# Swapped operands for the P product of twelve mLSTM units: values stationary, P streaming, the result turned back through DRAM

## The chip, the core and the metric

The kernel runs on one core of a Trainium2 chip. Its time is the device time of one execution in microseconds; the time of a version is the median of its runs. TensorE (PE in the profile) multiplies matrices into PSUM, with weight loads (PEld) as instructions of their own; VectorE (DVE), ScalarE (ACT) and GpSimd (POOL) do the element-wise work; SyncE (SP) issues most transfers (DMA).

## What is computed

An mLSTM cell over 4 batches, 8 heads, 768 steps and a head size of 40, followed by a wide MLP over its 3072 rows of 320 numbers. Everything is fp32. Cut to what matters:

```
for t in range(S):                                   # S = 768, for each of 4 x 8 heads
    m_new = max(f[t] + m, i[t])
    f_stab, i_stab = exp(f[t] + m - m_new), exp(i[t] - m_new)
    C = f_stab * C + i_stab * outer(v[t], k[t])      # 40 x 40
    n = f_stab * n + i_stab * k[t]                   # 40
    y[t] = sigmoid(o[t]) * (C @ q[t]) / max(abs(n @ q[t]), 1)
x = y as rows of (batch, step), 320 columns (8 heads x 40)
h = x @ w_in                                         # 320 -> 2048
out = (h - tanh(h)) @ w_out                          # 2048 -> 320
```

## The kernel before, in words

**Units.** The cell is done in chunks of 128 steps. A unit is one batch and one chunk with its 8 heads: 4 x 6 = 24 units, number n = chunk x 4 + batch. Within a unit, TensorE makes for each head the scores `ps` (keys against queries, 128x128, two heads at a time in the upper and lower 64 rows of the array), VectorE masks them into `P` (128 partitions are the source steps, the columns the target steps), and two kinds of products go into one PSUM tile `ph` (128 steps x 8 heads x 41; the 41st column is the denominator n·q):

- `inter` (line 654): what the state brings, three products per unit (three heads each, block-diagonal state), `ph<-state,q` in the profile;
- `intra` (line 663): what the steps of the chunk bring, one product per head, `ph<-vs,P`. `P` is the stationary operand (128x128), and the values `vs` of the head, scaled by the input gate in `scaled` (line 607) and with the scale itself as 41st column, stream through: 41 columns.

`gate` (line 668) reads `ph` on VectorE, makes the denominator `den`, multiplies it into the opened output gate `o`, and writes `ys`. `turn_by_store` (line 726) turns `ys` in blocks of 32x32 on VectorE into `yt`, stores that to DRAM (`y_rows`, four transfers) and loads it back as `xT` (two transfers), so that features lie on partitions. `update` makes `pc`, three products of keys and values, and `keep_state` adds them to the state on VectorE.

**MLP.** Two units make a group of 256 rows; there are 12 groups. For each group and each of 8 pairs of 128-wide strips of the hidden layer, `up` makes `ph_up` from `xT` and `w_in` (320 = 128 + 128 + 64: the 64-row rests run in pairs in the halves of the array), ScalarE and VectorE form h - tanh(h) from polynomials (`z`, `q`, `gt`), and `down_seven` multiplies `gt` and its sums `s` with `w_out` and `wT` into `pS`, seven products in place of eight. An item is two pairs of one group.

**Order.** The kernel pins the order of every engine to the order of its calls. Units 0 to 11 and the first four groups are laid out by a planner (`Plan`) with costs and ranks. From the item START = 17 on, 32 items follow in a loop written out by hand. In each item TensorE gets the `ph_up` products (with other work merged in), then the 64-row rests together with the scores of a new unit (`halves`), then the `pS` products of the item before. The work of units 12 to 23 is laid beside it in slots of two items: slot `(s, s - 1)` begins unit s and finishes the unit o = s - 1 before it; `cell_slot` (line 743) lists its steps, `spread_over` spreads them evenly over the two items, and `merge` (line 1031) sets them between the items' own steps. Work that waits for another engine is put off by `Clock.later` by so many microseconds of planned time.

**Buffers.** The `ph_up` tiles have two PSUM banks, used by every item, so that VectorE's first pass over them (`gt<-ph_up,z`) must be over before the next item's products start. The scores have the banks `a0` and `a1` to themselves. `ph` and `pc` share one bank in these slots. `P` has four buffers in SBUF, `vs` four, `yt` two.

In the profile every instruction carries the line of a helper that pins the order (L129 for TensorE, L106 for the others), so that the names of the tiles tell what it is. An fp32 product appears as two records of matmul and two of weight load.

Of the kernel before, what the change touches and what calls it, by code (L numbers as in the profile page):

```python
# [49 lines left out]
FP = mybir.dt.float32  # L50
# [5 lines left out]
OP = mybir.AluOpType  # L56
# [4 lines left out]
L = 128  # L61
# [18 lines left out]
def kernel(  # L80
# [188 lines left out]
    B, NT, D, H, _ = qT.shape  # L269
# [72 lines left out]
    def load_unit(n, names=("kz", "qz", "v", "k", "o", "q2"), queue=SP, behind=()):  # L342
        c, b = divmod(n, B)
        t = ld.setdefault(n, {})
        for name in names:
            if name in ("kz", "qz"):
                t[name] = load.tile([128, HH, L], FP, name=name, tag=name, bufs=3)
                for i in range(2):
                    src = kT if name == "kz" else qT
                    dma = queue.dma_start(out=t[name][i * HALF:i * HALF + D], in_=src[b, c, :, i * HH:(i + 1) * HH])  # L350
                    if behind:
                        tc.add_manual_dep(dma.ins, behind[-1].ins.name, SYNC, reason="order of transfers")
            elif name == "k":
                if n + B < NU:
                    t["k"] = load.tile([L, WIDE, D], FP, name="k", tag="k", bufs=3)
                    queue.dma_start(out=t["k"].rearrange("p h d -> p (h d)"),
                                    in_=bass.AP(k.tensor, k[b, c].offset, [[H * D, L], [1, WIDE * D]]))
            elif name != "q2":
                src, bufs = {"v": (v, 3), "o": (o_gate, 4)}[name]
                t[name] = load.tile([L, H, D], FP, name=name, tag=name, bufs=bufs)  # L360
                queue.dma_start(out=t[name], in_=src[b, c])
            elif c:
                t["q2"] = load.tile([TOP, len(TRIOS), L], FP, name="q2", tag="q2", bufs=3)
                for i in range(TRIO):
                    queue.dma_start(out=t["q2"][i * D:(i + 1) * D, 0:len(range(i, H, TRIO))], in_=qT[b, c, :, slice(i, H, TRIO)])
# [210 lines left out]
    def trio(t, j):  # L576

        return t[:, TRIOS[j].start:TRIOS[j].stop].rearrange("p h d -> p (h d)")
# [18 lines left out]
    def prepare(n, whole=True, by_heads=False):  # L597

        t = un[n]
        if "vs" in t:  # L600
            return
        t["vs"] = scaled(n, 0, "vs", 4, by_heads)
        if whole:
            t["column"]()
            open_gate(n)

    def scaled(n, i, name, bufs, by_heads=False):

        t = un[n]
        to = att.tile([L, H, D1], FP, name=name, tag=name, bufs=bufs)  # L610
        scale = ei[:, i, t["c"], t["hs"]]
        t["column"] = lambda: A.copy(out=to[:, :, D], in_=scale)
        if by_heads:
            for h in range(H):
                A.mul(out=to[:, h, 0:D], in_=t["v"][:, h], mul=scale[:, h:h + 1])
        else:
            V.tensor_tensor(out=to[:, :, 0:D], in0=t["v"], in1=scale.unsqueeze(2).to_broadcast([L, H, D]), op=OP.mult)
        return to
# [32 lines left out]

    def inter(n, j):
        t = un[n]
        if "ph" not in t:
            t["ph"] = small([L, H, D1], "ph")
        if t["c"]:
            rows = slice(0, len(TRIOS[j]) * D)
            T.matmul(trio(t["ph"], j), t["qs"][rows, j, :], trio(state[t["b"]][t["c"] % 2][rows], j), start=(j == 0), stop=False,  # L660
                     skip_group_check=True)

    def intra(n, h):
        t = un[n]
        T.matmul(t["ph"][:, h, :], t["P"][:, h // HH, h % HH, :], t["vs"][:, h, :], start=(t["c"] == 0 and h == 0), stop=True,
                 skip_group_check=True)

    def gate(n, in_parts=False):

        t = un[n]  # L670
        ph, sg = t["ph"], t["o"]
        den = att.tile([L, H], FP, name="den", tag="den")


        def over():
            V.scalar_tensor_tensor(out=den, in0=ph[:, :, D], scalar=-1.0, in1=inv[:, t["c"], t["hs"]], op0=OP.mult, op1=OP.max)
            V.tensor_tensor(out=den, in0=den, in1=ph[:, :, D], op=OP.max)
            V.reciprocal(out=den, in_=den)

        def shares():  # L680
            for h in range(H):
                A.mul(out=sg[:, h], in_=sg[:, h], mul=den[:, h:h + 1])

        def product():
            y = t["y"] = ys[n % 2]
            V.tensor_tensor(out=y.rearrange("p (h d) -> p h d", d=D), in0=ph[:, :, 0:D], in1=sg, op=OP.mult)

        if in_parts:
            return over, shares, product
        over()  # L690
        V.tensor_tensor(out=sg, in0=sg, in1=den.unsqueeze(2).to_broadcast([L, H, D]), op=OP.mult)
        product()

    def update(n, j, at_once=True):
        t = un[n]
        if j == 0:
            t["pc"] = small([TOP, H, D1], "pc")
        T.matmul(trio(t["pc"], j), t["k"][:, TRIO * j:TRIO * (j + 1)].rearrange("p h d -> p (h d)"), trio(t.get("vs_end", t["vs"]), j), start=True, stop=True)
        if j == len(TRIOS) - 1 and at_once:
            keep_state(n)  # L700
# [25 lines left out]
    def turn_by_store(n):  # L726

        y, g, tt = un[n]["y"], *divmod(n, GT)  # L730
        yt = att.tile([L, NB, BLOCK], FP, name="yt", tag="yt")
        flat = yt.rearrange("p b j -> p (b j)")
        V.transpose(flat[:, 0:NK * 128], y[:, 0:NK * 128])
        V.transpose(flat[:, NK * 128:], y[:, FROM[NK]:])
        rows = dram.tile([(NK + 1) * 128, L], FP, name="y_rows", tag=f"y_rows{n % 4}")
        for a in range(L // BLOCK):
            part = slice(a * BLOCK, (a + 1) * BLOCK)
            SP.dma_start(out=rows[:, part].rearrange("(b i) j -> i b j", i=BLOCK), in_=yt[part])
        for i in range(2):
            half = slice(i * HALF, (i + 1) * HALF)  # L740
            SP.dma_start(out=xT[g % NX][half, :, tt * L:(tt + 1) * L], in_=rows.rearrange("(c p) t -> p c t", p=128)[half])

    def cell_slot(s, o):


        steps, pause = [], [(0.0, lambda: None)]
        if o is not None:
            prepare(o)
        if s is not None:
            if s + 1 < NU and s + 1 not in ld:  # L750
                load_unit(s + 1)
            begin(s)
        if o is None:
            return [(0.0, lambda: prepare(s))]
        for d, heads in enumerate(TRIOS):
            steps.append((0.22 if o >= B else 0.0, lambda d=d: inter(o, d)))
            steps += [(0.22, lambda h=h: intra(o, h)) for h in heads]
        steps.append((0.0, lambda: gate(o)))
        steps += 5 * pause
        if o + B < NU:  # L760
            steps += [(0.2, lambda j=j: update(o, j)) for j in range(len(TRIOS))] + 4 * pause
        steps += [(0.0, lambda: turn_by_store(o))] + 2 * pause
        if s is not None:
            steps.append((0.0, lambda: prepare(s)))
        return steps + 2 * pause


    gT, po = {}, {}
# [624 lines left out]
        spread_over([(0.0, lambda p=p: [step() for _, step in sums_of_weights(p)])], START + p / 2, START + 0.5 + p / 2)  # L1393
    banks[:] = [name for name in ("b0", "b1") if name != third["tag"]]
    load_unit(PLANNED)
    for x in range(START, len(items) + LAG):
        dense, new = [], []
        for slot, x0, x1 in begins[x]:
            spread_over(cell_slot(*slot), x0, x1)
            if slot[0] is not None:  # L1400
                new.append(slot[0])
        if x < len(items):
            some = tuple(run[:2] for run in items[x])
            dense, rest = up(some, shrink(x))
            dense.append((0.6 + 0.9 * len(new[:1]), lambda: halves(rest, *(scores(n) for n in new[:1]))))
        dense += [(0.9, lambda n=n: halves(scores(n))) for n in new[1 if x < len(items) else 0:]]
        some = tuple(run[:2] for run in items[x - LAG])
        if in_seven(*some[0]):
            dense += down_seven(some)
        else:  # L1410
            for i, run in enumerate(items[x - LAG]):
                dense += down(i, some, *run)
        if x == len(items):
            dense.insert(4, (0.0, count))
            dense.insert(13, (0.0, load_count))
        merge(dense, [(at - x, cost, step) for at, cost, step in sorted(work[x], key=lambda w: w[0])])

    Clock.tick(100.0)
# [197 lines left out]
```

## Time and profile before

| | us |
|---|---|
| runs | 542.87, 531.3, 532.08 |
| median | 532.08 |
| the profiled execution: its own time | 542.49 |
| its span in the trace | 540.7 |
| TensorE busy in the span | 534.0 |
| VectorE busy | 361.5 |
| ScalarE busy | 199.8 |
| GpSimd busy | 35.8 |
| eight score products of a unit, first to last start of record and length | 218.21 to 219.20 |
| units 12 to 23: first scores to last product | about 214 to 472 |

The page of the profile gives for each engine the time in which one of its instructions ran. Matmuls are pipelined: the recorded length of one (0.3 to 0.4 us for the products here) reaches over the start of the next, so what a product costs TensorE is read from the starts of successive lines in the timeline and not from the length of a line. A line of the timeline merges consecutive records of one kind; its columns are start, length, engine, source line, operation, `output<-inputs`, shape and number of records.

### The profile page before, as it was taken

The numbers are of one execution on the slowest core, as the hardware profiler recorded it, in microseconds if no ns is written. First come the engines' busy times: TensorE is split into PE (matmuls) and PEld (weight loads), VectorE is DVE, ScalarE is ACT, GpSimd is POOL, SyncE is SP. The second block draws the span as 40 slices with busy tenths as digits, with TensorE's granted clock in tenths as the row PEclk, the third lists the DMA queues.
The fourth block names the chain that finished last, engine by engine and source line by source line (L and its number), as shares of the span: only waits on it lengthen the run. The fifth ranks groups of instructions, "written<-read, shape, count | busy, mean of one in ns | idle before, by whom it ended". The sixth has DMA issues, their size and how long they took to land.

```text
span 540.7 us, 9346 instructions
## 1 busy us (share of the span) xinstructions
PE 534.0 (99%) x3505; PEld 464.4 (86%) x3505; DVE 361.5 (67%) x792; ACT 199.8 (37%) x509; POOL 35.8 (7%) x63
## 2 busy tenths in 40 slices
PE   9999999999999999999999999999999999999996
PEld 5778888788888988898899899989989989988885
DVE  3678979998766557765756657557566566555544
ACT  4157487576543433232232242223223223222312
POOL 4421312310000000000000000000000000000000
PEclk9999999999999999999999999999999999999999
DMA  7966456551201000002132241241231221020001
GB/s 231 273 193 201 134 141 186 159 161 57 79 16 62 1 26 24 1 26 70 59 105 46 60 130 25 80 115 16 76 94 38 76 54 16 16 53 1 25 0 31
DMA packets 52331, 42.71 MB, mean 79 GB/s; under 512 B 23160, under 2 KB 46008, under 8 KB 52280
## 3 DMA queue, kind: packets, MB, share of 16 engines
q1 hardware_dynamic: 46048, 27.29, 18.8%
q0 software_dynamic: 3040, 10.82, 6.4%
q10 hardware_dynamic: 3192, 3.93, 2.1%
q8 instruction: 30, 0.49, 0.4%
q14 instruction: 21, 0.17, 0.1%
HBM read 35.73 MB, written 6.29 MB: 78 GB/s over the span
## 4 chain that ended last, share of the span: by engine, by line
PE 98%; ACT 1%; DVE 0%; issue 0%
PE ph_up L129 41%; PE pS L129 30%; PE ph L129 10%; PE po L129 7%; PE ps L129 5%; PE awake L129 3%; PE pc L129 2%; PE px L133 1%; ACT vs L106 0%; PE gate L129 0%; ACT L106 0%; PE gate L133 0%; DVE ob L106 0%; ACT part L106 0%; ACT o L106 0%; ACT ei L106 0%
## 5 line engine op out<-in xcount | busy, mean ns | idle before, releaser
L129 PE MATMUL ph_up<-xT,w_in 128*128 128x256 f32 (+1 forms) x1152 | 243.9, 391 | 0.0
L129 PEld LDWEIGHTS ph_up<-xT,w_in 128*128 128x128 f32 (+1 forms) x1152 | 169.5, 189 | 30.7 <-issue 14.3
L106 ACT ACTIVATE z<-ph_up 128x512 f32<-128x512 f32 (+1 forms) x98 | 56.8, 583 | 256.7 <-PE ph_up L129 139.2
L106 DVE SCALAR_TENSOR_TENSOR gt<-ph_up,z 128x512 f32<-128x512 f32 (+1 forms) x98 | 63.5, 675 | 70.7 <-ACT z L106 70.3
L129 PE MATMUL pS<-wT,s 128*128 128x160 f32 x480 | 73.8, 301 | 0.0
L129 PEld LDWEIGHTS pS<-wT,s 128*128 128x128 f32 x480 | 67.6, 190 | 0.0
L106 ACT ACTIVATE q<-z,tiny 128x512 f32<-128x512 f32 (+1 forms) x98 | 66.2, 711 | 1.0
L106 DVE TENSOR_TENSOR P<-ps,upto 128x512 f32<-128x512 f32 x36 | 23.2, 685 | 64.3 <-PE ps L129 64.3
L129 PEld LDWEIGHTS ph<-vs,P 128*128 128x128 f32 x384 | 59.8, 203 | 5.1 <-issue 1.2
L106 DVE SCALAR_TENSOR_TENSOR gt<-q,gt 128x512 f32<-128x512 f32 (+1 forms) x98 | 63.4, 681 | 0.0
L129 PE MATMUL ph<-vs,P 128*128 128x41 f32 x384 | 57.7, 272 | 0.0
L129 PE MATMUL pS<-w_out,gt 128*128 128x160 f32 x320 | 56.4, 313 | 0.0
L129 PEld LDWEIGHTS pS<-w_out,gt 128*128 128x128 f32 x320 | 45.0, 190 | 8.8 <-issue 5.6
L129 PE MATMUL po<-w_out,gt 128*128 128x320 f32 x128 | 38.2, 441 | 0.0
L129 PEld LDWEIGHTS po<-w_out,gt 128*128 128x128 f32 x128 | 23.1, 190 | 8.5 <-issue 0.3
L106 DVE TENSOR_TENSOR s<-gt 128x256 f32<-128x256 f32 x80 | 30.2, 418 | 0.0
L129 PE MATMUL pS<-wT,gt 128*128 128x160 f32 x160 | 29.6, 304 | 0.0
L129 PEld LDWEIGHTS ps<-qz,kz 40*128 40x128 f32 x384 | 27.6, 205 | 2.2 <-DVE vs L106 0.8
L129 PE MATMUL ps<-qz,kz 40*128 40x128 f32 x384 | 28.7, 293 | 0.0
L129 PE MATMUL pS<-w_out,s 128*128 128x160 f32 x160 | 28.3, 300 | 0.0
L129 PEld LDWEIGHTS pS<-w_out,s 128*128 128x128 f32 x160 | 23.9, 190 | 0.0
L129 PEld LDWEIGHTS pS<-wT,gt 128*128 128x128 f32 x160 | 23.8, 190 | 0.0
(94 smaller groups left out, 468.7 us busy)
## 6 DMA issues: line engine op xcount, KB each, us to landing
w<-in_moe_w_out POOLq DMA_DIRECT2D x8, 640.0 KB, 5.2
w<-in_moe_w_in POOLq DMA_DIRECT2D x16, 256.0 KB, 4.8
kz<-in_kT SPq DMA_DIRECT2D x48, 80.0 KB
o<-in_o_gate SPq DMA_DIRECT2D x24, 160.0 KB
k<-in_k SPq DMA_DIRECT2D x20, 180.0 KB
qz<-in_qT SPq DMA_DIRECT2D x44, 80.0 KB
v<-in_v SPq DMA_DIRECT2D x22, 160.0 KB
out<-ob ACTq DMA_DIRECT2D x11, 320.0 KB
```

The source lines that it names most:

```text
L106: i = method(*args, **kwargs)
L129: return cls.keep(nc.tensor.matmul(*args, **kwargs))
L133: return cls.keep(nc.tensor.transpose(*args, **kwargs))
```

## The change

For units 12 to 23 the product of P and the values changes its operands' roles. The values of a head become the stationary operand: 64 columns of the tile `vs`, taken from column h x 41, so that 41 of them belong to the head and the other 23 to the next one (the tile is 23 columns longer, and these are set to zero). `P` streams through, 128 columns. Even and odd products go to the two column halves of the array, two heads at a time, and their results to the upper and lower 64 partitions of the tile `pT`, in the bank `a1`. All eight stand together, in the item after the one with the scores.

The result has the values on partitions and the steps in columns. `turn_back` turns it on VectorE in blocks of 32x32 (`zt`), stores the blocks to DRAM (`h_rows`, four transfers) and loads them in another order (`z_in`, four transfers), so that steps lie on partitions again. `ph` then holds only what the state brings; `gate_turned` adds `z_in` to it on VectorE in two instructions (the first 32 of the 41 columns, and the other 9) and goes on as before with the sum `both`. `zt` and `z_in` take buffers of `P`; `yt` has one buffer instead of two.

`cell_slot` lists its steps in a new order: the state update of the unit before first, then the scaling of the new unit's values, then the three state products, the gate and the turn.

The diff, cut to its core:

```diff
     def scaled(n, i, name, bufs, by_heads=False):
-        to = att.tile([L, H, D1], FP, name=name, tag=name, bufs=bufs)
+        flat = att.tile([L, H * D1 + HALF - D1], FP, name=name, tag=name, bufs=bufs)
+        to = flat[:, 0:H * D1].rearrange("p (h d) -> p h d", d=D1)
+        t["wide"] = flat
...
-    def inter(n, j):
+    def inter(n, j, stop=False):
...
-    def gate(n, in_parts=False):
+    def gate(n, in_parts=False, den=None):
...
-        yt = att.tile([L, NB, BLOCK], FP, name="yt", tag="yt")
+        yt = att.tile([L, NB, BLOCK], FP, name="yt", tag="yt", bufs=1)
...
+    def intra_turned(n):
+        t = un[n]
+        if "turned" not in t:
+            G.memset(t["wide"][:, H * D1:], 0.0)
+            t["turned"] = ps_a.tile([128, HH, L], FP, name="pT", tag="a1")
+        for j in range(HH):
+            for i in range(2):
+                h = i * HH + j
+                T.matmul(t["turned"][i * HALF:(i + 1) * HALF, j, :], t["wide"][:, h * D1:h * D1 + HALF], t["P"][:, i, j, :],
+                         start=True, stop=True, skip_group_check=True)
+
+    def turn_back(n):
+        t = un[n]
+        zt = att.tile([128, HH * L // BLOCK, BLOCK], FP, name="zt", tag="P", bufs=4)
+        V.transpose(zt.rearrange("p b i -> p (b i)"), t["turned"].rearrange("p j t -> p (j t)"))
+        rows = dram.tile([2, 2, HH, L, BLOCK], FP, name="h_rows", tag=f"h_rows{n % 4}")
+        for a in range(128 // BLOCK):
+            half, low = divmod(a, 2)
+            SP.dma_start(out=rows[low, half].rearrange("j (b k) i -> k (j b) i", k=BLOCK), in_=zt[a * BLOCK:(a + 1) * BLOCK])
+        t["z"] = att.tile([L, 2, H, BLOCK], FP, name="z_in", tag="P", bufs=4)
+        for i in range(4):
+            part = slice(i * BLOCK, (i + 1) * BLOCK)
+            SP.dma_start(out=t["z"][part].rearrange("t a h i -> t (a h) i"),
+                         in_=rows.rearrange("a c j t i -> t (a c j) i")[part])
+
+    def gate_turned(n):
+        t = un[n]
+        both = att.tile([L, H, D1], FP, name="both", tag="both", bufs=1)
+        ph, sg = t["ph"], t["o"]
+        den = att.tile([L, H], FP, name="den", tag="den")
+
+        def share():
+            V.tensor_tensor(out=sg, in0=sg, in1=den.unsqueeze(2).to_broadcast([L, H, D]), op=OP.mult)
+
+        t["ph"] = both
+        over, _, product = gate(n, in_parts=True, den=den)
+        return [
+            lambda: V.tensor_tensor(out=both[:, :, 0:BLOCK], in0=ph[:, :, 0:BLOCK], in1=t["z"][:, 0], op=OP.add),
+            lambda: V.tensor_tensor(out=both[:, :, BLOCK:], in0=ph[:, :, BLOCK:], in1=t["z"][:, 1, :, 0:D1 - BLOCK], op=OP.add),
+            over, share, product]
+
     def cell_slot(s, o):
...
-        for d, heads in enumerate(TRIOS):
-            steps.append((0.22 if o >= B else 0.0, lambda d=d: inter(o, d)))
-            steps += [(0.22, lambda h=h: intra(o, h)) for h in heads]
-        steps.append((0.0, lambda: gate(o)))
-        steps += 5 * pause
         if o + B < NU:
-            steps += [(0.2, lambda j=j: update(o, j)) for j in range(len(TRIOS))] + 4 * pause
-        steps += [(0.0, lambda: turn_by_store(o))] + 2 * pause
+            steps += [(0.2, lambda j=j: update(o, j)) for j in range(len(TRIOS))] + 3 * pause
         if s is not None:
             steps.append((0.0, lambda: prepare(s)))
-        return steps + 2 * pause
+        steps += 5 * pause
+        steps += [(0.22, lambda d=d: inter(o, d, True)) for d in range(len(TRIOS))] + pause
+        gates = []
+        steps.append((0.0, lambda: [gates.extend(gate_turned(o)), gates[0]()]))
+        steps += [(0.0, lambda i=i: gates[i]()) for i in range(1, 5)]
+        steps.append((0.0, lambda: turn_by_store(o)))
+        return steps + 4 * pause
...
+    news = []
     for x in range(START, len(items) + LAG):
-        dense, new = [], []
+        dense, new, scored = [], [], news
...
             dense.append((0.6 + 0.9 * len(new[:1]), lambda: halves(rest, *(scores(n) for n in new[:1]))))
+            for n in scored:
+                dense.append((0.9, lambda n=n: [intra_turned(n), Clock.later("turned", 1.2, lambda: turn_back(n))]))
...
+        news = new
```

On the engines' order this gives, for each of the twelve units: on TensorE eight `pT<-P,vs` products between the `ph_up` rests and the `pS` products of one item, in place of eight `ph<-vs,P` products spread over an item's `ph_up` and `pS` products; on VectorE one turn of 128x512 and two additions more; on SP eight transfers more, after those of `turn_by_store` and ahead of the next unit's loads; on GpSimd one fill of 128x23.

More of the change, by code (lines that the diff above doesn't have):

```diff
@@ L659, in inter @@
             rows = slice(0, len(TRIOS[j]) * D)
-            T.matmul(trio(t["ph"], j), t["qs"][rows, j, :], trio(state[t["b"]][t["c"] % 2][rows], j), start=(j == 0), stop=False,
+            T.matmul(trio(t["ph"], j), t["qs"][rows, j, :], trio(state[t["b"]][t["c"] % 2][rows], j), start=(j == 0), stop=stop,
                      skip_group_check=True)
@@ L666, in intra @@
                  skip_group_check=True)
-    def gate(n, in_parts=False):
+    def gate(n, in_parts=False, den=None):
         t = un[n]
         ph, sg = t["ph"], t["o"]
-        den = att.tile([L, H], FP, name="den", tag="den")
+        den = den or att.tile([L, H], FP, name="den", tag="den")
         def over():
@@ L741, in turn_by_store @@
             SP.dma_start(out=xT[g % NX][half, :, tt * L:(tt + 1) * L], in_=rows.rearrange("(c p) t -> p c t", p=128)[half])
+    def intra_turned(n):
[34 more added lines that the diff above has]
+            over, share, product]
     def cell_slot(s, o):
         steps, pause = [], [(0.0, lambda: None)]
-        if o is not None:
-            prepare(o)
         if s is not None:
```

## The prediction

> **What bounds the kernel now.** I read the page first, then the stretch in which the change acts, then the waits of that stretch, then TensorE's timeline item by item, and last the DMA queue of SP. The page shows one busy engine and a chain that runs through it almost alone:
>
> ```profile
> span 540.7 us, 9346 instructions
> PE 534.0 (99%) x3505; PEld 464.4 (86%) x3505; DVE 361.5 (67%) x792; ACT 199.8 (37%) x509; POOL 35.8 (7%) x63
> PE 98%; ACT 1%; DVE 0%; issue 0%
> ```
>
> Units 12 to 23, the only ones the change touches, run from about 214 us (first scores of unit 12) to 472 us (end of unit 23). The windows view of that stretch, and its longest waits by VectorE (columns: who waited for whom, total us, times, longest):
>
> ```profile
> 205.00:475.00 270.00, 270.00 (x1873) 244.20 (x1872) 174.09 (x395) 72.50 (x188) 0.00 (x0) 1.00 0.21 56
> DVE P L106 <- PE ps L129: 59.9, 12, 5.4
> DVE gt L106 <- ACT z L106: 23.5, 15, 5.1
> ```
>
> TensorE is busy all 270 of 270 us; VectorE has 174 and waits for the others, not they for it; DMA uses 0.21 of its engines. So the time of this stretch is the sum of what TensorE has to do, and an edit is worth what it changes there as long as nobody makes TensorE wait.
>
> What does a unit cost TensorE? Every fp32 product is two records. An MLP item (two pairs: 12 products of `ph_up`, 14 of `pS`) without a unit is the length from one `ph_up` to the next:
>
> ```profile
> 205.17 4.68 PE L129 MATMUL ph_up<-xT,w_in 128*128 128x256 f32 x24
> 213.69 4.68 PE L129 MATMUL ph_up<-xT,w_in 128*128 128x256 f32 x24
> 218.21 1.06 PE L129 MATMUL ps<-qz,kz 40*128 40x128 f32 x16
> 223.10 1.24 PE L129 MATMUL ph_up<-xT,w_in 128*128 128x256 f32 x5
> ...
> 461.31 1.03 PE L129 MATMUL ph_up<-xT,w_in 128*128 128x256 f32 x4
> ...
> 463.26 0.31 PE L129 MATMUL ph<-vs,P 128*128 128x41 f32 x2
> 463.40 0.68 PE L129 MATMUL ph_up<-xT,w_in 128*128 128x256 f32 x2
> 463.92 0.31 PE L129 MATMUL ph<-vs,P 128*128 128x41 f32 x2
> ...
> 465.01 0.38 PE L129 MATMUL ph<-state,q 120*128 120x123 f32 x2
> 465.23 1.67 PE L129 MATMUL ph_up<-xT,w_in 128*128 128x256 f32 x10
> ...
> 469.50 0.35 PE L129 MATMUL ph<-state,q 80*128 80x82 f32 x2
> 469.68 0.75 PE L129 MATMUL pS<-wT,s 128*128 128x160 f32 x4
> ...
> 472.07 1.24 PE L129 MATMUL ph_up<-xT,w_in 128*128 128x256 f32 x5
> ```
>
> A plain item: 213.69 - 205.17 = 8.52. An item with only the scores of a unit (unit 12): 223.10 - 213.69 = 9.41, so eight score products cost 0.89. The item of unit 23 holds all eight products of P and the values and two of the three state products: 472.07 - 461.31 = 10.76, which is 2.24 over a plain one. The state products take 465.23 - 465.01 = 0.22 and 469.68 - 469.50 = 0.18. Left for the eight P products: 2.24 - 0.40 = 1.84, or 0.23 each. The lines at 463 us show where that goes: the product itself takes 0.14 (463.26 to 463.40) although it streams only 41 columns, and the `ph_up` product behind it takes 0.52 instead of 0.43 (463.40 to 463.92). Its own streaming would be 41/256 of 0.43, or 0.07: the rest is weight loads that the short stream cannot cover.
>
> **What the skill says.** First, the Trainium skill, "TensorE: Matmul & The Clock Gate", section "LDWEIGHTS (loading the stationary operand)": the load's time goes with the columns of the stationary operand. The trace agrees as far as it can show: P as stationary (128 columns) loads in 190 ns per record, and the 41-column product is dearer than its stream. Second, the Trainium skill, "TensorEngine Tiling (Array Packing)", section "When to Use Tiling": a moving operand of at most 64 columns is a reason to swap the operands and tile the columns in two. No row of this trace tiles columns. The nearest is the scores, tiled in two halves of the rows: eight products of 128 columns would stream 8 x 128/256 x 0.43 = 1.72 one after the other, and cost 0.89, so fp32 halves of the rows do run side by side here. Third, the same page, "Key Properties": a change of tiling mode drains the array. `ph_up` in this trace has such changes (64-row halves after full rows), and the item has them before and after alike; my estimate for one is 0.10, from 4.61 (205.17 to 209.78, where `pS` begins) less 8 x 0.43 and 2 x 0.43 of streaming, 0.31, of which at most a third is put to each change and to the last drain.
>
> **The change part by part.** Removed: the eight products `ph<-vs,P` of a unit, 1.84. Added: eight products `pT<-P,vs` with 64 columns stationary and 128 streaming, alternately to the upper and lower half. They stand where no score product stands (the item after the scores), between the half-row products of `ph_up` and the `pS` products. If the two column halves run side by side as the row halves of the scores do, they cost 0.89, plus one more mode change, 0.10: 0.99. Both sides of this unknown: not below the pure stream of 0.86 without any drain; no overlap at all gives 1.72 + 0.10 and edges of 0.04, 1.86; if each change of half also drained, 8 x (0.215 + 0.10) + 0.10 = 2.6. I take 0.99, since the same engine overlaps the same size of product in the same precision in this trace.
>
> Moved: the three state products no longer have P products around them; one stands in the last `pS` products of an item, two in the next `ph_up`. Their 0.22, 0.22 and 0.18 stay; I add 0.04 for edges, as a state product ahead of `pS` shows in other slots. The state update `pc` keeps its place among `ph_up` products and its cost. So a unit saves 1.84 - 0.99 - 0.04 = 0.81, and twelve save 9.7.
>
> VectorE gets: the turn of `pT`, 128x512 (from `yt<-ys` 128x256 at 438 ns and 128x128 at 269 ns, a slope that makes 0.78), two additions (128x256 as `s<-gt`, 0.42; 128x72 about as `den<-den,ph` of 0.16, say 0.2): 1.4 a unit, 17 in all, on 174 of 270. It is hidden as long as the two `gt<-ph_up,z` instructions that free the `ph_up` banks are in time. VectorE keeps program order, and in the item with `pT` it has behind the end of `ph_up`: first `gt`, `ys` 0.49, `yt` 0.44 + 0.27, second `gt`, then the turn. First `gt` can start 0.87 after `pS` could (ScalarE's `z`: 290.83 to 291.70 in the slot before), so the second ends at about 0.87 + 0.68 + 1.20 + 0.68 = 3.4. TensorE has 0.99 + 3.91 of `pT` and `pS` before it needs the first bank and 1.7 more before the second: 1.5 or more in hand. In the item with scores, `vs` (0.48) may come before the two masks and `gt`: 1.0 + 2 x 0.69 + 0.48 + 2 x 0.68 = 4.2 against 4.8, again covered, with the second bank needed later still. If that cover went, each microsecond would cost 12.
>
> The new wait is VectorE's addition on `z`, the product that came back through DRAM; behind it in VectorE's queue stand the gate, and then the next `gt` of `ph_up`, for which TensorE waits. The queue of SP now has for each unit, in this order, four stores of `yt`, two loads of `xT`, four stores of `zt`, four loads of `z`, and then the loads of the next unit. The trace has the first two:
>
> ```profile
> 248.07 1.86 SPq L106 DMA_DIRECT2D y_rows<-yt  x4
> 251.43 1.33 SPq L106 DMA_DIRECT2D xT<-y_rows  x2
> 252.86 0.85 SPq L106 DMA_DIRECT2D kz<-in_kT  x2
> ```
>
> Four stores issue in 1.86 and land 1.5 later (249.93 to 251.43). `zt` has 16/12 of the pieces, so 2.5 for four; from the end of `yt` at 2.7 after `ph_up`: 1.9 + 1.5 + 1.3, then 2.5 + 1.5 + 2.5 and an estimated 2 to land: 15.9. The addition comes after the last state product of the item after next: 0.99 + 3.91 + 0.22, one item of 10.3, and 1.4: about 16.8. If `z` is later than that, 3 more pass before the next `gt` is late (`ph_up` ends 3.2 later, ScalarE needs 0.87, the gate 1.6), and 1.5 more before TensorE stands. So `z` is some 5 before it costs anything. The bytes, 0.5 MB a unit on DMA engines that are 0.21 busy, cost nothing.
>
> The rest costs nothing: the 23-column memset lies on POOL, which is idle in this stretch (0.00 busy), `vs` is scaled earlier in the slot with its load a slot ahead, `yt` in one buffer is rewritten 20 us later, and the finished `y` leaves at about the same place of its slot, two items before its group.
>
> **The sum.** The profiled execution took 542.49 (540.7 of span and 1.8 around it), 10.4 above the median of 532.08. In the stretch that matters TensorE has no gap and items repeat to the hundredth, so the saving holds in microseconds for either: 542.49 would become 532.8, and the median 532.08 - 9.7 = 522.4.
>
> **The rivals.** (a) The column halves don't run side by side: 1.86 in place of 0.99 takes back 0.87 x 12 = 10.4, to 532.8, no change. For it: the trace has no column tiling, and both halves need all 128 rows for their loads. Against: the scores. (b) Slower: each `pT` product waits for its own weight loads, because the next load is not pulled ahead while the other half streams. At the record's 190 ns beside a stream of 107, sixteen records cost 16 x 0.297 = 4.75 a unit, 3.8 more than forecast, 45 in all: 567. With half of each load hidden it is 16 x 0.202 = 3.2, or 549. It makes the kernel slower from 1.80 a unit on, and by 2% from 2.7. (c) `z` or the turn comes so late that the bank of `ph_up` is freed late: the gain is gone at 0.81 of stall a unit, that is with `z` some 6 later than I work out; at 2 of stall it would be 522.4 + 24 = 546. Against it: 35% of VectorE free and the 5 in hand.
>
> **How the numbers follow.** Forecast 0.66, at 519.5 to 525; (a) or something between, 0.19, at 525 to 535; (b) 0.08 and (c) 0.07, half of these past 543. About 2% either way, 10.6, is what a measurement of this kernel can tell from no change. The forecast lies at 1.8%, 0.9 short of that bound: a `pT` of 0.91 crosses it, so almost half of its chance, 0.31, goes to faster; slower gets 0.09 and the rest, 0.60, is within 2%. The range 519.5 to 536 leaves out (b) and the worse part of (c), and a little of the good side.
>
> **What would show it.** Right: items with `pT` about 1.0 + 0.40 over 8.52, 16 `pT` records in about 0.9 with starts in pairs a few ns apart, TensorE still 100% in the stretch. Wrong: starts of `pT` evenly 107 ns apart (a) or 200 and more (b), TensorE idle before `ph_up` on `gt`, or VectorE idle before `both` on a DMA for over 5 us (c).

## The result, and the profile after

| | before | after |
|---|---|---|
| median of the first comparison, us | 532.23 | 529.77 |
| ratio, first comparison | | 0.9869 [0.9823, 0.9914] |
| median of a second comparison, us | 532.5 | 523.27 |
| ratio, second comparison | | 0.982 [0.9777, 0.9863] |
| a profiled execution: own time and span | 531.2, 529.5 | 525.33, 523.5 |
| stretch of units 12 to 23 in it | 258.38 | 249.27 |

The changed kernel is faster by 1.3% in the first comparison and by 1.8% in the second, and the two intervals overlap. The ratios leave out executions that took about 10 us more, which both kernels have (three of the six behind the median of 529.77, two of the six behind 532.23); in the two that were traced, the prediction's profile of the kernel before and the profile of the longest detour below, units 12 to 23 begin at 213.69 and 213.87 in place of the 202.5 to 205.2 of all other profiles.

The page of the changed kernel shows the same picture as before, with a little more on VectorE (the second line is busy time per engine, the third the chain):

```profile
span 523.5 us, 9566 instructions
PE 515.2 (98%) x3505; PEld 445.5 (85%) x3505; DVE 375.7 (72%) x828; ACT 199.7 (38%) x509; POOL 37.5 (7%) x75
PE 96%; DVE 1%; ACT 1%; POOL 1%; DMA 0%; issue 0%; SPq 0%; DVEq 0%
```

The windows view, from the first scores of unit 12 to the end of unit 23 (us; then busy time and instructions of PE, PEld, DVE, ACT, POOL; clock; share of the DMA engines; GB/s):

```profile
205.13:454.40 249.27, 249.27 (x1806) 222.37 (x1805) 178.13 (x408) 69.18 (x179) 0.94 (x8) 1.00 0.39 89
```

TensorE is still busy in all of it, so the stretch is again the sum of its products. VectorE is busy 178 of 249, and DMA 0.39 of its engines.

TensorE's timeline around two items of the last units, where no state update is mixed in, gives the new price of a unit:

```profile
386.32 4.68 PE L129 MATMUL ph_up<-xT,w_in 128*128 128x256 f32 x24
390.83 1.06 PE L129 MATMUL ps<-qz,kz 40*128 40x128 f32 x16
...
396.41 4.68 PE L129 MATMUL ph_up<-xT,w_in 128*128 128x256 f32 x24
401.02 1.09 PE L129 MATMUL pT<-P,vs 128*64 128x128 f32 x16
402.04 1.35 PE L129 MATMUL pS<-w_out,gt 128*128 128x160 f32 x8
...
405.95 1.24 PE L129 MATMUL ph_up<-xT,w_in 128*128 128x256 f32 x5
```

The second item is 405.95 - 396.41 = 9.54 long, 1.02 over a plain one of 8.52; the eight swapped products stand at 401.02 to 402.04, and nothing else is in it. The first is 396.41 - 386.32 = 10.09, 1.57 over a plain one: 0.89 for the scores as before, and 0.68 for the three state products. A unit thus costs 1.02 + 1.57 = 2.59. Before, two items with one unit's work among them took from 420.54 to 440.92 in the first profile:

```profile
420.54 1.03 PE L129 MATMUL ph_up<-xT,w_in 128*128 128x256 f32 x4
...
432.19 4.68 PE L129 MATMUL ph_up<-xT,w_in 128*128 128x256 f32 x24
...
440.92 1.03 PE L129 MATMUL ph_up<-xT,w_in 128*128 128x256 f32 x4
```

That is 11.65 + 8.74, or 3.35 over two plain ones. The saving is 0.76 a unit and 9.1 for twelve, which is what the two stretches differ by: 258.38 - 249.27 = 9.11.

### The profile page after: what moved, and what is told of

The parts are those of the page before. It is cut to its first block, busy times and chain, and to the rows that moved or that the text cites. A ratio compares the mean times of both kernels' runs of the same rounds, so it can differ in the third digit from the quotient of the medians.

```text
span 523.5 us, 9566 instructions
## 1 busy us (share of the span) xinstructions
PE 515.2 (98%) x3505; PEld 445.5 (85%) x3505; DVE 375.7 (72%) x828; ACT 199.7 (38%) x509; POOL 37.5 (7%) x75
## 4 chain that ended last, share of the span: by engine, by line
PE 96%; DVE 1%; ACT 1%; POOL 1%; DMA 0%; issue 0%; SPq 0%; DVEq 0%
PE ph_up L129 41%; PE pS L129 31%; PE po L129 7%; PE ph L129 6%; PE ps L129 4%; PE pT L129 2%; PE pc L129 2%; PE awake L129 1%; PE px L133 1%; DMA w_out<-in_i_gate 0%; POOL w L106 0%; ACT vs L106 0%; DVE w_in L106 0%; PE gate L129 0%; ACT L106 0%
## 5 line engine op out<-in xcount | busy, mean ns | idle before, releaser
L129 PE MATMUL ph_up<-xT,w_in 128*128 128x256 f32 (+1 forms) x1152 | 232.6, 388 | 0.0
L129 PEld LDWEIGHTS ph_up<-xT,w_in 128*128 128x128 f32 (+1 forms) x1152 | 173.4, 189 | 34.1 <-issue 15.3
L129 PE MATMUL pS<-w_out,gt 128*128 128x160 f32 x320 | 55.0, 312 | 0.0
L129 PEld LDWEIGHTS ps<-qz,kz 40*128 40x128 f32 x384 | 25.5, 188 | 2.4 <-DVE vs L106 0.8
L129 PE MATMUL ps<-qz,kz 40*128 40x128 f32 x384 | 26.4, 274 | 0.1
L129 PEld LDWEIGHTS ph<-vs,P 128*128 128x128 f32 x192 | 23.9, 192 | 1.3 <-POOL P L106 0.9
L129 PE MATMUL ph<-vs,P 128*128 128x41 f32 x192 | 24.4, 273 | 0.4 <-POOL P L106 0.4
```

The source lines that it names most:

```text
L129: return cls.keep(nc.tensor.matmul(*args, **kwargs))
```

## The experiments

**The kernel before, and the change, once more.** The first comparison showed 7.0 us where the stretch of the trace had lost 9.1. Nothing was edited in these two.

> The kernel before, unchanged, to see its own spread and its start. In its stretch of units 12 to 23 (first scores to the end of unit 23) every theory expects 258.4 us again, as in its first profile. My theory of the missing 2 us (the change saved 9.1 in that stretch of the trace, and 7.0 of the median): the start before unit 12 varies from run to run by some us in both kernels, so this kernel against itself shows a ratio whose interval is about as wide as that of the change, and starts of 202 to 214 us. The rival, that the change lengthens the start of its kernel: this kernel's starts agree within 1 us and lie near 203.

> The changed kernel once more, for a narrower interval. If the start only varies, the ratio moves to 0.983 (9.1 of 532). If the change also lengthens the start or the end by 2 us, it stays at 0.987. The stretch itself is 249.3 us in both cases, with 16 records of the swapped product in 1.02 us.

Measured: the kernel before against itself 1.0006 [0.9975, 1.0037]; the change 0.982 [0.9777, 0.9863]. The stretches are 258.38 and 249.27 again. Where they begin can be read from TensorE's timeline, the `ph_up` line that opens the item with unit 12's scores. In the kernel before, in its new profile, with the line that follows unit 23:

```profile
202.52 0.81 PE L129 MATMUL ph_up<-xT,w_in 128*128 128x256 f32 x3
...
460.90 2.32 PE L129 MATMUL ph_up<-xT,w_in 128*128 128x256 f32 x10
```

In the changed kernel it begins at 205.13 in one profile and here, in the second, at:

```profile
203.72 1.46 PE L129 MATMUL ph_up<-xT,w_in 128*128 128x256 f32 x6
```

Of the kernels below, three with the swapped products begin at 202.59, 202.75 and 202.80, one at 205.04, and the one with the old operands at 205.18. So the start, which the change leaves as it was, varies by some 2.6 us between executions, with the old operands as with the new, and nothing here says that the change lengthens it. That is as large as the difference between the first comparison and the stretch; what makes the start vary stays open. The second comparison lies nearer to what the trace says, and the first agrees with it inside its interval.

**Do the halves overlap, and is that the gain?** The order of the eight products changed, four to the upper half and then four to the lower:

```diff
-        for j in range(HH):
-            for i in range(2):
+        for i in range(2):
+            for j in range(HH):
```

> The changed kernel with the eight swapped products in another order: four heads to the upper column half, then four to the lower, so that neighbours are in the same half and can't run beside each other. My theory (the halves overlap, and that is where the gain comes from): 16 records in about 1.72 - 0.11 + 0.13 = 1.75 us in place of 1.02, items 0.73 longer, 12 x 0.73 = 8.8 us slower than the change, so about the time of the kernel before. The rival (the gain comes from grouping and from loads of 64 columns in place of 128, with no overlap): unchanged, within 1 us of the change.

Then all eight put to the upper half:

```diff
-                T.matmul(t["turned"][i * HALF:(i + 1) * HALF, j, :], t["wide"][...], t["P"][:, i, j, :],
+                T.matmul(t["turned"][0:HALF, j, :], t["wide"][...], t["P"][:, i, j, :],
...
-        V.transpose(zt..., t["turned"]...)
+        V.transpose(zt[0:HALF]..., t["turned"][0:HALF]...)
...
-            SP.dma_start(out=rows[low, half]..., in_=zt[a * BLOCK:(a + 1) * BLOCK])
+            SP.dma_start(out=rows[low, half]..., in_=zt[low * BLOCK:(low + 1) * BLOCK])
```

> The changed kernel with all eight swapped products in the upper column half; the second head of each pair overwrites the first, and what the lower half would hold is left out (the stores send the upper half twice, so the transfers are as many). It prices the case of no overlap. My theory (overlap of the halves is the whole gain): 16 records at 0.109 us, 1.74 and edges of 0.1, so 1.84 in place of 1.02, the stretch 12 x 0.82 = 9.8 us longer, about 533, a ratio of 1.00 to the kernel before. The rival (the shorter weight loads bring part of the gain by themselves): 529 or less.

Measured: four and four 528.14 (0.9925 [0.9883, 0.9967]); all in one half 533.68 (1.0018 [0.9985, 1.0051]). The same item as above, first with four and four, then with one half, each with the line of the swapped products and the next:

```profile
403.06 1.58 PE L129 MATMUL pT<-P,vs 128*64 128x128 f32 x16
404.57 1.35 PE L129 MATMUL pS<-w_out,gt 128*128 128x160 f32 x8
```

```profile
406.27 1.96 PE L129 MATMUL pT<-P,vs 128*64 128x128 f32 x16
408.16 1.35 PE L129 MATMUL pS<-w_out,gt 128*128 128x160 f32 x8
```

Eight products take 1.02 in alternation, 1.51 as four and four, and 1.89 in one half. Without overlap the swap is worth nothing: 1.89 against the 1.84 of the old operands, and a stretch of 259.66 against 258.38. The whole gain is the overlap of the two column halves, and the rival that the loads of 64 columns help by themselves falls. It is not enough that products go to both halves; neighbours in the queue should: with four and four, 0.49 of the 0.87 a unit that the overlap brings is lost. My expectation for it, 1.75 and 8.8 us in all, missed: the stretch grew by 5.8, since the halves still overlapped in part, which the last section takes up.

The Trainium skill, "TensorE: Matmul & The Clock Gate", section "Measured speedup vs the span model", has 2.38 times for three column tiles; here two column halves in fp32 give 1.89 / 1.02 = 1.85 times, near the factor of 2 that "TensorEngine Tiling (Array Packing)", section "Theoretical Speedup", names as the most.

**Is it the grouping?** The kernel before, with the old operands, but with its eight P products in one step:

```diff
-        for d, heads in enumerate(TRIOS):
-            steps.append((0.22 if o >= B else 0.0, lambda d=d: inter(o, d)))
-            steps += [(0.22, lambda h=h: intra(o, h)) for h in heads]
+        steps += [(0.22, lambda d=d: inter(o, d)) for d in range(len(TRIOS))] + 4 * pause
+        steps += [(1.76, lambda: [intra(o, h) for h in range(H)])] + 3 * pause
```

> The kernel before with the old operands (P stationary), but the eight P products of a unit together in one step in place of spread between the products of the MLP. My theory: what the old product costs is its two weight loads of 128 columns[...], so eight take 1.70 us together as in the start of the kernel, and 1.84 when spread: 12 x 0.14 = 1.7 us faster than before, and no more. The rival (most of the gain came from no longer cutting into the MLP's products): close to the changed kernel, 6 us or more faster than before.

Measured: 544.17, a ratio of 1.019 [1.0111, 1.0269], slower, which neither theory expected. Its timeline, from an item with the P products to the next, and the stall after it:

```profile
267.63 1.03 PE L129 MATMUL ph_up<-xT,w_in 128*128 128x256 f32 x4
...
273.59 1.98 PE L129 MATMUL ph<-vs,P 128*128 128x41 f32 x16
275.39 1.33 PE L129 MATMUL pS<-w_out,gt 128*128 128x160 f32 x8
...
279.28 1.46 PE L129 MATMUL ph_up<-xT,w_in 128*128 128x256 f32 x6
281.61 0.44 PE L129 MATMUL pc<-vs,k 128*120 128x123 f32 x2 [0.87 <-DVE ys L106]
```

The eight products take 1.80 together (273.59 to 275.39), and the item, with the scores and two state products in it, is 279.28 - 267.63 = 11.65 long, just as the item at 420.54 in the kernel before, which has the same content with the eight spread. So grouping saves nothing, and the 1.70 that I read off the start of the kernel did not carry over. The loss is another matter: the P products now come late in their slot, the gate on VectorE after them, and the state update `pc`, which shares its bank with `ph`, waits for `ys` to have read it. In all eight slots that have a `pc`, TensorE stands 0.83 to 0.88 before it, and it starts 0.10 to 0.15 after the end of `ys`. The stretch is 8.7 longer than before, 1.1 for each of these slots. The order that the change gives does not run into this wait, and nor did the order before; whether the swapped products would have done as well in the old order was not tried.

**Is the way through DRAM hidden?** First left out:

```diff
+        t["zt"] = zt
...
-        rows = dram.tile([2, 2, HH, L, BLOCK], FP, name="h_rows", tag=f"h_rows{n % 4}")
-        (four stores from zt, four loads to t["z"])
...
-            lambda: V.tensor_tensor(out=both[:, :, 0:BLOCK], in0=ph[:, :, 0:BLOCK], in1=t["z"][:, 0], op=OP.add),
+            lambda: V.tensor_tensor(out=both[:, :, 0:BLOCK], in0=ph[:, :, 0:BLOCK], in1=t["zt"]...[:, 0], op=OP.add),
```

> The changed kernel without the way through DRAM: the eight transfers of a unit are left out, and VectorE adds the turned tile as it lies, so the values of the result are those of other places. My theory (the trip is hidden, and VectorE's part stays): the same stretch of 249.3 us, and the time of the change within 1 us. The rival (transfers on SP, or the wait for them, cost something): 1 to 3 us faster than the change.

Then made longer, by two and by four transfers within DRAM for each unit:

```diff
+        for hop in range(2):
+            again = dram.tile([2, 2, HH, L, BLOCK], FP, name="h_rows", tag=f"h_again{hop}_{n % 4}")
+            SP.dma_start(out=again, in_=rows)
+            rows = again
         t["z"] = att.tile([L, 2, H, BLOCK], FP, name="z_in", tag="P", bufs=4)
```

> The changed kernel with two more transfers of the whole 256 KB within DRAM between the stores and the loads of each unit, about 3 to 4 us each, so that the product comes back some 7 us later. In the trace of the change it lies ready about 2 us before VectorE asks for it, VectorE then has 2.6 us of idle time before its next pass over the MLP's result, and TensorE asks for the bank 2 to 3.6 us after that. My theory: a wait of about 5 us in VectorE's rows for each unit, and 0 to 1 us of it on TensorE, 523 to 534 in all. The rival, that TensorE feels every microsecond that the product is late: 12 x 5 = 60 us slower.

> The same with four such transfers, some 14 us later. My theory: past the point where VectorE's idle time and the bank's cover are used up (about 7 us), each microsecond of delay is one of TensorE, about 6 to 7 a unit, 12 x 6 = 70 us slower than the change, with TensorE idle before the MLP's products. The rival, that the order of two items per unit gives more room than I count: under 20 us slower.

Measured: without it 523.88 (0.981 [0.9724, 0.9897]), the stretch 249.26; with two transfers more 557.28 (1.0435 [1.0338, 1.0533]); with four 624.83 (1.1695 [1.1542, 1.1848]). So the trip of the change costs TensorE nothing, its transfers included. In the first profile of the change VectorE stood once for it (who, for whom: total us, times, longest):

```profile
DVE both L106 <- DMA z_in<-h_rows: 0.8, 1, 0.8
```

A longer trip does cost, and with two more transfers far more than the 523 to 534 that I expected. The waits over 200 to 490 us there, in the same columns (in the two units of the second line the profile names another transfer):

```profile
DVE both L106 <- DMA z_in<-h_rows: 66.3, 10, 9.0
DVE both L106 <- DMA qz<-in_qT: 14.3, 2, 7.6
PE pS L129 <- DVE ob L106: 10.0, 2, 5.3
PE ph_up L129 <- DVE gt L106: 8.7, 7, 2.0
```

and one unit of it on VectorE and TensorE:

```profile
261.32 0.56 DVE L106 TENSOR_TENSOR both<-ph,z_in 128x256 f32<-128x256 f32 x2 [5.65 <-DMA z_in<-h_rows]
...
262.97 0.68 DVE L106 SCALAR_TENSOR_TENSOR gt<-ph_up,z 128x512 f32<-128x512 f32 x1
```

```profile
263.71 1.13 PE L129 MATMUL ph_up<-xT,w_in 128*128 128x256 f32 x4 [1.08 <-DVE gt L106]
```

VectorE waits 5.65 for the product; the gate and the next `gt` stand behind it, and TensorE waits 1.08 for the bank that this `gt` frees. So of this wait about 4.6 is covered, and the rest is TensorE's. The waits for `ob` show a shorter cover that I had not counted: where a group ends, the sums `ob` that empty the `pS` banks stand behind the same addition. In one unit VectorE waited 8.65 for `z_in` and TensorE 4.69 for `ob`, so that 4.0 was covered:

```profile
442.51 0.42 DVE L106 TENSOR_TENSOR both<-ph,z_in 128x256 f32<-128x256 f32 x1 [8.65 <-DMA z_in<-h_rows]
442.85 0.48 DVE L106 TENSOR_TENSOR ob<-pS,a 128x320 f32<-128x320 f32 x1
```

```profile
443.39 2.50 PE L129 MATMUL pS<-w_out,gt 128*128 128x160 f32 x8 [4.69 <-DVE ob L106]
445.68 1.27 PE L129 MATMUL pS<-wT,gt 128*128 128x160 f32 x4
```

These lines show a second cost. The eight `pS` products behind the wait take 2.29 (443.39 to 445.68), while the same eight take 1.19 in the changed kernel (402.04 to 403.23 above). The windows view gives TensorE's granted clock as 0.50 from 443.39 to 446.75. Over the whole stretch of units 12 to 23, with two transfers more:

```profile
202.75:478.80 276.05, 259.25 (x1807) 229.10 (x1806) 177.49 (x408) 69.39 (x179) 0.94 (x8) 0.97 0.43 100
```

The stretch is 26.8 longer than the 249.27 of the change. TensorE stands for 16.8 of that, and for the other 10.0 it is busy longer with the same products. The item behind the stretch, which finishes unit 23 and holds the other wait for `ob`, takes 16.1 in place of 8.5. Together these are 34.4, and the kernel as a whole is 34.0 slower than the change (557.28 against 523.27). My expectation counted only the first of these three parts, and put it at 0 to 1 a unit where it was 1.4.

The step from two to four transfers costs 624.83 - 557.28 = 67.6, or 5.6 a unit. From its first store to its last load a unit's trip takes 6.1 in the change, 12.3 with two transfers and 18.1 with four (means of the twelve units), so that four bring it back 5.7 later than two do. Past the cover, then, a unit pays about as much as the delay, but not by standing alone: the mean granted clock of an execution also falls, from 0.98 with two to 0.93 with four. The trip of the change stands close to its edge on VectorE, which waited 0.8 in one unit; TensorE has a cover of about 4 more.

## Why the prediction was right

The forecast was 522.4 with TensorE's sum as the reason; the second comparison gave 523.27, and the first 529.77 with a ratio of 1.3%, in the range of 519.5 to 536 and within 2% of before.

The first median, of all six executions, lies in the band from 525 to 535 that was given to rival (a). It is the trace, with 0.76 of 0.81 a unit saved, that decides for the forecast and against (a). That 523.27 comes within 1 us of 522.4 is in part luck, as the start alone varies by 2.6.

- *TensorE's sum sets the time of the stretch.* Shown: busy 249.27 of 249.27 after, and the stretch falls by what the products fall.
- *Removed: 1.84 a unit.* It stands: 3.35 for the unit less 0.89 of scores and 0.62 of state products. The eight grouped products cost the same in their item. That weight loads make up what the 41 columns don't explain is still a reading: no run changes the loads of the old products alone.
- *Added: 0.99.* Measured 1.02. Its mode change, put at 0.10, shows in the starts: 0.306 from the last half-row record to the first swapped one, against 0.209 from one pair of half-row records to the next. The step that carried the forecast, that column halves in fp32 overlap as row halves do, was an analogy with the scores, without a row for column tiling; it held, and the kernel with all eight in one half shows that all of the gain hangs on it. Rival (a), no overlap, was put at 532.8 and measured 533.68.
- *State products: 0.62 + 0.04.* Measured 0.68, as in the last units all three stand among `pS` products (0.68 = 1.57 - 0.89). Together with the 0.03 above this makes 0.76 in place of 0.81 a unit, 9.1 in place of 9.7.
- *VectorE's added work is hidden.* Shown: TensorE has no gap; the turn took 0.70 (0.78 estimated), the additions 0.42 and 0.22 (0.42 and 0.2).
- *`z` comes in time, with about 5 in hand.* The trip is hidden, as leaving it out shows. The four stores and four loads of the turned product took 5.9 from the first issue to the end of the last in the second unit (248.06 to 253.97 on SP's queue), against 6.5 worked out. The cover of a late `z` was put at 3 and 1.5 after VectorE begins to wait. The 3 is a slip: its own terms, 3.2 + 0.87 - 1.6, make 2.5, and the "some 5" in hand holds with it. The longer trip shows 5.65 - 1.08 = 4.57, against 4.0. The prediction missed two things here: the group's end, where `ob` waits behind the addition, and that TensorE's products can run slower behind a wait. The change as made comes to neither. But rival (c) was priced too low: with `z` some 6 later the gain was to be just gone, and with it 6.2 later than in the change the kernel took 557.28, 25 over the kernel before.
- *Rival (b)*, loads that are not pulled ahead, is excluded by the 1.02, which leaves no room for them.

## What to carry to other kernels

When TensorE has no gaps, price an edit by lengths from one start to the next in otherwise equal stretches: the recorded length of a 41-column product here, 0.31 for two records, is not what it cost, 0.23. Swapping the operands of a product with a narrow moving side bought nothing by itself here; it paid because two halves of the array then ran side by side, so send neighbouring products to different halves. A result that takes a detour costs nothing while it is back in time. Before lengthening it, look at everything that stands in program order behind the instruction that waits, at group ends as well as in the plain case, and allow for slower products behind a wait of TensorE.

## What the runs showed of the hardware

Products that go to one column half alone start 0.109 us apart per record (128 columns streamed in fp32, two records a product; the kernel with all eight in one half). When the halves alternate in the queue, as in the change, the records start in pairs, 6 to 7 ns apart within a pair and 0.109 from pair to pair. The tile view of the changed kernel has the loads and products:

```profile
L129 PEld LDWEIGHTS pT<-P,vs x192: 132/137/137, 219.2 to 441.0; 128*64 128x64 f32 x192
L129 PE MATMUL pT<-P,vs x192: 272/273/324, 219.2 to 441.1; 128*64 128x128 f32 x192
```

A load of 64 columns is recorded at 137 ns, against 190 for 128 columns in the profile before: fewer columns, a shorter record, but 0.72 of the time for half the columns. The loads of both halves are taken ahead, while products of the same rows run: in the first unit the second pair of loads starts at 219.21, between the first pair of products at 219.16 and the second at 219.32.

TensorE's granted clock can fall behind a wait. With two transfers more, both waits of over 4.6 us were followed by a clock of 0.50 for some microseconds, and products of 160 columns then took nearly twice as long. Behind the shorter waits it differed: after two of 1.49 and 1.29 us close together (at 352.80 and 354.53) it stayed at 1.00, and at two of 1.25 and 1.28 (at 376.11 and 377.84) it fell to 0.50 from 377.2 to 384.0. In the kernel with the old operands grouped, the waits of up to 0.88 left it at 1.00.

With four products to one half and then four to the other, the first unit's 16 records start at 216.82, 216.98 and then every 0.11 up to 217.31, where two start 5 ns apart; from there on about every 0.055 until 217.69, and again every 0.11 until 218.13. Read as two series of eight records, each with a first gap of 0.16 and then 0.109, the second half's series begins at 217.31, when three records of the first half, which precede it in the program, had not started. The Trainium skill, "TensorE: Matmul & The Clock Gate", section "The mechanism", says that matmuls start strictly in program order; the starts here suggest a few records of room between the halves. The records don't name the half, so this is a reading of the pattern and not shown; that four and four takes 1.51 and not the 1.75 or more of halves one after the other is measured.
